# Seven half products for eight in the last 1024 tokens of a forgetting-attention and feed-forward kernel, and a new order of all its operations

## The chip, the cores and the metric

One core of one Trainium2 chip runs the whole program. It has five engines with queues of their own: TensorE (PE in the profile, with PEld for its weight loads), VectorE (DVE), ScalarE (ACT), GpSimd (POOL) and SyncE (SP), which issues most of the DMAs. The metric is the time of the program on the device in microseconds, the median of several runs.

## The reference

Eight batches of eight heads, 576 tokens and 64 channels go through a causal attention with a decay that is a running sum of log f; its output, 4608 tokens of 512 channels, goes through a feed-forward part with two in-projections that are multiplied element by element. In short:

```python
scores = (q @ k.T) / 8 + cum[:, None] - cum[None, :]     # cum = cumsum(log f); -1e9 above the diagonal
attn = softmax(scores)
x = (attn @ v), heads side by side                        # 4608 x 512
a, b = x @ w_a, x @ w_b                                    # 512 x 1536 each
out = (a * b) @ w_out                                      # 1536 x 512
```

## The kernel before

Everything is computed in f16 with f32 sums. The kernel first builds a list of some 2350 operations, each with an engine (or a choice of engines), an assumed duration and what it depends on, and then emits them in an order that is written out in the code: `ORDER` (L1212) is that order, found by a planner, `CHOICE` (L1324) a letter for each operation that may run on more than one engine (D, A, P for DVE, ACT, POOL), and `SLOTS` (L141) the buffer of its ring that each taker of a ring gets. Each engine runs its own operations strictly in that order, so an operation that waits holds all that stands behind it on its engine.

Attention (`attention`, L822) runs for 32 pairs of heads, four to a batch. For a pair: PE forms the scores in PSUM (tile `sc`), DVE adds the decay and takes the row maximum (L674), ACT takes the exponential and its sum (L701, L705), DVE the reciprocal (L713, L715), POOL or ACT multiplies by it (L726, L724; tiles `PA` and `PB`). A DMA transpose issued by SP turns the result (`do_tr`, L736, into `PTA` and `PTB`), PE multiplies it with v (L769, L784, tile `pvx`), and DVE or ACT puts that into `xT`, the feed-forward part's input: four tiles of 128 channels by 4608 tokens. The decay rows (`spread`) come by DMA or by PE.

The feed-forward part (`ffn`, L1124) walks over tiles of tokens, `cuts` (L1206): 256, 256, 256, 384, six of 512, 384. For each of 12 blocks of 128 hidden channels PE forms `psa` and `psb` (`ff_mm`, L1056), ACT copies the first to `a16`, DVE multiplies the second with it into `ht`. A group for 512 tokens is 8 PE instructions, four blocks of 128 input channels in two halves of 64 hidden channels (`mm_halves`, L72). Then, for each 128 tokens, PE forms the output in three groups of 8 (`ff_out`, L1078, tile `pso`), DVE or ACT copies it out, SP stores it. The very last 128 tokens go in three pieces (`psz`). The PSUM ring of the feed-forward part has four buffers (`ff`), that of the scores two of two banks (`sc`).

A tile of `ffn` can start once the attention output of all its tokens is in `xT`. The order spreads these products between the attention's own on PE. "wake" products (L79) fill PE at the start, before there is work for it.

## Time and profile before

| | us |
|---|---|
| runs before | 401.96, 400.78, 397.33 |
| median | 400.78 |
| span of the profiled execution | 397.5 |
| PE busy in it | 386.4 |
| DVE, ACT, POOL busy in it | 293.0, 290.6, 257.8 |

The profiled execution is one of its own; beside its span no time is given for it. In the views, a row of the timeline or of the chain of waits has its start, its length, engine, line, operation, output and inputs, shape and a count; a row of groups has a count, the busy time and the mean of one, and the idle time of the engine in front of them with what ended it; a row of windows has the stretch, then for PE, PEld, DVE, ACT and POOL the busy time with the number of instructions, the granted clock, the share of the DMA engines and GB/s. Nearly all feed-forward products carry the line of their helper, L74, so they are told apart by the tiles' names.

### The profile page before, as it was taken

The numbers are of one execution on the slowest core, as the hardware profiler recorded it, in microseconds if no ns is written. First come the engines' busy times: TensorE is split into PE (matmuls) and PEld (weight loads), VectorE is DVE, ScalarE is ACT, GpSimd is POOL, SyncE is SP. The second block draws the span as 40 slices with busy tenths as digits, with TensorE's granted clock in tenths as the row PEclk, the third lists the DMA queues.
The fourth block names the chain that finished last, engine by engine and source line by source line (L and its number), as shares of the span: only waits on it lengthen the run. The fifth ranks groups of instructions, "written<-read, shape, count | busy, mean of one in ns | idle before, by whom it ended". The sixth has DMA issues, their size and how long they took to land.

```text
span 397.5 us, 14691 instructions
## 1 busy us (share of the span) xinstructions
PE 386.4 (97%) x5768; PEld 250.9 (63%) x5768; DVE 293.0 (74%) x971; ACT 290.6 (73%) x805; POOL 257.8 (65%) x464
## 2 busy tenths in 40 slices
PE   6899999999999999999999999999999999999997
PEld 3557887969766665655555665555555556567785
DVE  7888798999998779787888798668878772333131
ACT  5999899999879778778988588898878763232131
POOL 8689687769887679884996877779936871000000
PEclk9999999999999999999999999999999999999999
DMA  7999999999999999999999999999999586100202
GB/s 117 256 195 167 157 147 226 220 285 283 244 188 228 238 293 234 235 249 292 231 205 278 223 255 214 248 258 206 252 220 230 104 147 156 63 2 1 81 28 81
DMA packets 147365, 76.87 MB, mean 193 GB/s; under 512 B 124384, under 2 KB 128352, under 8 KB 147296
## 3 DMA queue, kind: packets, MB, share of 16 engines
q1 hardware_dynamic: 132856, 68.72, 77.7%
q0 software_dynamic: 14256, 7.08, 14.7%
q8 instruction: 45, 0.74, 0.8%
q14 instruction: 24, 0.20, 0.2%
q10 hardware_dynamic: 184, 0.14, 0.1%
HBM read 52.05 MB, written 9.58 MB: 155 GB/s over the span
## 4 chain that ended last, share of the span: by engine, by line
PE 77%; DMA 11%; POOL 4%; ACT 3%; issue 2%; DVE 2%; SPq 0%; DVEq 0%; ACTq 0%; POOLq 0%
PE psa L74 21%; PE psb L74 20%; PE pso L74 20%; PE sc L551 4%; DMA PTA<-PA 3%; PE pvx L769 3%; POOL PA L726 2%; DMA PTB<-PB 2%; PE psT L359 2%; DMA wb<-in_moe_w_b_dram 2%; PE sc L539 2%; DMA wout<-in_q_dram 2%; PE sc L74 1%; PE psP L74 1%; DMA k<-in_k_dram 1%
## 5 line engine op out<-in xcount | busy, mean ns | idle before, releaser
L674 DVE CUSTOM_DVE_ANT_0 S<-sc,spread 64x576 f32<-64x576 f32 (+4 forms) x232 | 125.9, 562 | 17.3 <-ACT PA L705 8.3
L74 PE MATMUL psb<-xT,wb 128*64 128x512 f16 (+2 forms) x1056 | 113.9, 341 | 0.8 <-DMA wb<-in_moe_w_b_dram 0.5
L74 PE MATMUL psa<-xT,wa 128*64 128x512 f16 (+2 forms) x1056 | 114.1, 341 | 0.0
L289 ACT CAST a<-psa 128x512 f16<-128x512 f32 (+1 forms) x114 | 63.3, 559 | 56.4 <-PE psa L74 52.3
L1073 DVE TENSOR_TENSOR ht<-psb,a 128x512 f16<-128x512 f32 (+1 forms) x114 | 74.4, 658 | 38.5 <-PE psb L74 27.7
L74 PE MATMUL pso<-wout,ht 128*64 128x512 f16 x840 | 102.4, 380 | 0.0
L726 POOL TENSOR_SCALAR PA<-PA,st 128x256 f16<-128x256 f16 (+2 forms) x180 | 84.9, 483 | 8.8 <-DVE st L715 5.5
L705 ACT ACTIVATE PA<-S,st 128x256 f16<-128x256 f32 (+2 forms) x168 | 84.2, 504 | 6.5 <-DVE st L674 6.0
L74 PEld LDWEIGHTS <-wb 128*64 128x64 f16 x1056 | 62.5, 110 | 30.0 <-issue 2.5
L74 PEld LDWEIGHTS <-wa 128*64 128x64 f16 x1056 | 61.7, 110 | 29.3 <-issue 2.2
L726 POOL TENSOR_SCALAR PB<-PB,st 128x512 f16<-128x512 f16 (+1 forms) x90 | 63.4, 711 | 24.3 <-DVE st L715 10.7
L74 PEld LDWEIGHTS <-ht 128*64 128x64 f16 x912 | 49.9, 110 | 33.0 <-issue 1.9
L705 ACT ACTIVATE PB<-S,st 128x512 f16<-128x512 f32 x56 | 40.2, 720 | 3.3 <-DVE st L674 3.0
L705 ACT ACTIVATION_READ_ACCUMULATOR PA<-S,st 128x1 f32 x168 | 32.1, 191 | 0.0
L701 ACT ACTIVATE PB<-S,st 128x576 f16<-128x576 f32 x28 | 21.7, 775 | 9.8 <-POOL PA L726 3.1
L631 POOL TENSOR_SCALAR_AFFINE_SELECT spread<-spread 128x768 f32<-128x768 f32 x24 | 20.9, 870 | 10.1 <-DMA spread<-cum_d 10.0
L769 PEld LDWEIGHTS <-nv 128*64 128x64 f16 x640 | 21.7, 110 | 7.5 <-DMA PTA<-PA 2.1
L674 DVE CUSTOM_DVE_ANT_1 S<-sc,spread 128x256 f32<-128x256 f32 x48 | 19.8, 419 | 6.9 <-PE sc L539 2.0
L715 DVE RECIPROCAL st<-st 128x2 f32<-128x2 f32 x128 | 18.3, 156 | 6.9 <-ACT PB L705 3.5
L674 DVE DVE_READ_ACCUMULATOR2_ANT st<- 128x1 f32 (+1 forms) x280 | 23.0, 82 | 0.0
L551 PE MATMUL sc<-kT,qT 64*128 64x512 f16 (+4 forms) x144 | 20.8, 326 | 1.2 <-ACT kT L289 0.4
L289 ACT COPY osb<-pso 128x512 f32<-128x512 f32 x24 | 13.8, 580 | 9.1 <-PE pso L74 7.8
(106 smaller groups left out, 483.2 us busy)
## 6 DMA issues: line engine op xcount, KB each, us to landing
spread<-cum_d SPq DMA_DIRECT2D x24, 576.0 KB, 6.4
out_dram<-osb SPq DMA_DIRECT2D x35, 256.0 KB, 3.4
q<-in_q_dram SPq DMA_DIRECT2D x14, 576.0 KB, 5.7
k<-in_k_dram SPq DMA_DIRECT2D x14, 576.0 KB, 5.0
v<-in_v_dram SPq DMA_DIRECT2D x24, 256.0 KB, 6.0
wout<-in_moe_w_out_dram POOLq DMA_DIRECT2D x3, 512.0 KB, 7.5
nv<-in_v_dram POOLq DMA_DIRECT2D x8, 128.0 KB, 5.1
wa<-in_moe_w_a_dram POOLq DMA_DIRECT2D x2, 512.0 KB, 7.5
```

The source lines that it names most:

```text
L74: nc.tensor.matmul(out=out[r], lhsT=lhsT[:, r], rhs=rhs, **kw)
L289: nc.scalar.copy(out=out_, in_=in_)
L359: nc.tensor.matmul(out=p[m][HP[j] if quad else slice(0, 128), 64 * t:64 * t + 64], lhsT=x[r, j, t, :] if quad else x[r, t, :], rhs=ident16 ...
L551: nc.tensor.matmul(out=dst, lhsT=lhsT, rhs=rhs, start=start, stop=stop, skip_group_check=True)
L631: nc.gpsimd.affine_select(out=c[:, :, 0:SM].rearrange("p h (j k) -> p h j k", k=128), in_=c[:, :, SM:2 * SM].rearrange("p h (j k) -> p h j ...
L674: nc.vector.tensor_tensor_reduce(out=o, in0=x, in1=y, scale=-1.0, scalar=3e38, op0=ADD, op1=MIN, accum_out=m)
L701: nc.scalar.activation(out=p_blocks(t, 4), in_=T[("s" if direct else "z", t, 4)], func=EXP, bias=st[:, 8:9], scale=sign, accum_out=st[:, 1 ...
L705: nc.scalar.activation(out=p_blocks(t, i)[:, :, h, :], in_=(T[("s", t, i)][:, h, :] if direct else T[("z", t, i)][:, h * n:h * n + n]).rea ...
L715: nc.vector.reciprocal(out=st[:, 20 + 2 * i:22 + 2 * i], in_=st[:, 10 + 2 * i:12 + 2 * i])
L726: VEC[e].tensor_scalar(out=p, in0=p, scalar1=st[:, c:c + 1], scalar2=1.0, op0=MUL, op1=MUL)
L769: nc.tensor.matmul(out=o[HP[h], 128 * i:128 * i + 128], lhsT=vt[:, j, pr + NP * h, :], rhs=pt[:, base_blk[i] + 2 * block_at(t, i, j) + h, ...
L1073: nc.vector.tensor_tensor(out=ht[:, 0:n_], in0=T.pop(("psb", t0, fbs))[:, 0:n_], in1=T.pop(("a16", t0, fbs))[:, 0:n_], op=MUL)
```

## The change

Two things. First, the last 1024 tokens leave `ffn`: `cuts` ends at 3584, as 256, 256, 256, 384, four of 512 and 384, and the rest is done by `winograd()`. There the two weights (rows), the two halves of 512 tokens (columns) and the two halves of the 512 input channels (the inner dimension) are taken as a 2 x 2 block product, and in place of its eight half products seven are formed, from sums of the blocks. Sums of the weights (`sub_w`) are written over parts of `xT` that earlier tiles have used, one of them in place; sums of x (`add_x`) over a fourth part, one in place. The results are put together by copies out of PSUM (`snap`) and by sums and products on DVE and POOL (`combine`). A half product of a block of 128 hidden channels is 4 PE instructions. The output step is the same as before, now a function of its own (`out_step`).

Second, `ORDER`, `CHOICE` and `SLOTS` are all new; with them go other places of the same operations in every queue, and other engines for some. The number of operations goes from 2353 to 2463.

```diff
-    cuts = [256, 256, 256, 384] + [512] * 6 + [384]
+    cuts = [256, 256, 256, 384] + [512] * 4 + [384]
...
+    assert t0 == TW[0]
+    winograd()
...
+    def hidden(t0, fb, tb):
+        if t0 == TW[0]:
+            t0, tb = TW[tb // 4], tb % 4
+        return T[("ht", t0, fb)][:, 128 * tb:128 * tb + 128]
...
+    TW = (NT - 1024, NT - 512)
+    WCOL = 2 * DF
+
+    def w_sum(k):
+        return xTflat[k][:, 0:WCOL].rearrange("p (i c) -> p i c", i=2)
+
+    def x_sum(k, d):
+        c = 512 * (2 * k + d)
+        return xTflat[3][:, c:c + 512]
+
+    def sub_w(e, k, c):
+        a, b = wa16[:, :, c], wb16[:, :, c]
+        out_, x, y = ((w_sum(0), b[:, 0:2], a[:, 0:2]), (w_sum(1), b[:, 2:4], w_sum(0)[:, :, c]),
+                      (w_sum(2), a[:, 2:4], w_sum(1)[:, :, c]), (None, b[:, 2:4], b[:, 0:2]))[k]
+        VEC[e].tensor_tensor(out=b[:, 0:2] if out_ is None else out_[:, :, c], in0=x, in1=y, op=SUB)
+
+    def add_x(e, k, d):
+        p, q_, u, w = (xTflat[m][:, t:t + 512] for m, t in ((d, TW[0]), (2 + d, TW[0]), (d, TW[1]), (2 + d, TW[1])))
+        out_, x, y, op = ((x_sum(0, d), u, w, ADD), (x_sum(1, d), x_sum(0, d), p, SUB),
+                          (u, p, u, SUB), (x_sum(2, d), q_, x_sum(1, d), SUB))[k]
+        VEC[e].tensor_tensor(out=out_, in0=x, in1=y, op=op)
+
+    def product(m, fb):
+
+        f = slice(128 * fb, 128 * fb + 128)
+        if m == 1:
+            T[("wg", fb)] = ff_tile([128, 512], FP32, "wg")
+        if m == 2:
+            T[("wb", fb)] = slot(ps, [128, 2, 512], FP32, "sc", "wb")
+        o = T[("wb", fb)][:, int(m != 2), :] if m in (2, 3, 5) else T[("wg", fb)]
+        for d in range(2):
+            w = {1: wa16[:, d, f], 2: wa16[:, 2 + d, f], 3: wb16[:, 2 + d, f], 4: w_sum(2)[:, d, f],
+                 5: w_sum(0)[:, d, f], 6: w_sum(1)[:, d, f], 7: wb16[:, d, f]}[m]
+            x = {1: xTflat[d][:, TW[0]:TW[0] + 512], 2: xTflat[2 + d][:, TW[0]:TW[0] + 512], 3: x_sum(2, d),
+                 4: xTflat[2 + d][:, TW[1]:TW[1] + 512], 5: x_sum(0, d), 6: x_sum(1, d),
+                 7: xTflat[d][:, TW[1]:TW[1] + 512]}[m]
+            mm_halves(o, w, x, start=(d == 0 and m in (1, 2, 5)), stop=(d == 1), skip_group_check=True)
+
+    def snap(e, m, fb):
+        if m == 1:
+            T[("wu", fb)] = slot(n32_pool, [128, 2 * TG * 64], FP32, "n32", "wu")
+        if m == 5:
+            T[("wv", fb)] = slot(s_pool, [128, 1024], FP32, "S", "wv")
+        c = 512 * (m in (6, 7))
+        cast(e, T[("wu" if m in (1, 6) else "wv", fb)][:, c:c + 512], T[("wb", fb)][:, 1, :] if m == 5 else T[("wg", fb)], False)
+
+    def hidden_tile(half, fb):
+        if half:
+            key, n, tag = ("hx", fb // 3), fb % 3, "PA"
+            if key not in T:
+                T[key] = slot(p_pool, [128, 12, 128], FP16, "PA", "hx")
+        elif fb < 9:
+            key, n = ("hy", fb // 3), fb % 3
+            if key not in T:
+                T[key] = pt_pool.tile([128, 12, 128], FP16, tag="PTA", bufs=RING["PTA"], name="hy")
+        else:
+            x = T[("ht", TW[0], fb)] = slot(ht_pool, [128, 512], FP16, "ht", "ht")
+            return x
+        x = T[("ht", TW[half], fb)] = T[key].rearrange("p n k -> p (n k)")[:, 512 * n:512 * n + 512]
+        return x
+
+    def combine(e, what, fb):
+        u, w, g, be = (T.get((x, fb)) for x in ("wu", "wv", "wg", "wb"))
+        lo, hi = slice(0, 512), slice(512, 1024)
+        out_, x, y, op = {"c11": lambda: (u[:, lo], be[:, 0, :], u[:, lo], ADD),
+                          "c12": lambda: (u[:, hi], be[:, 1, :], u[:, hi], ADD),
+                          "c22": lambda: (w[:, hi], w[:, lo], g if fb in PLAIN else w[:, hi], ADD),
+                          "h1": lambda: (hidden_tile(0, fb), u[:, lo], u[:, hi], MUL),
+                          "h2": lambda: (hidden_tile(1, fb), g, w[:, hi], MUL)}[what]()
+        VEC[e].tensor_tensor(out=out_, in0=x, in1=y, op=op)
+
+    PLAIN = range(0, 12, 2)
+
+    def winograd():
+
+        seen = last_ff["in"]
+        n_in = [0]
+        for n in cuts:
+            n_in.append(n_in[-1] + 2 * 12 // max(1, min(4, 512 // n)))
+        free = [seen[n_in[-2] - 1]]
+        over = [seen[-1]]
+        need = [set(), set()]
+        for half in range(2):
+            for tok in range(TW[half], TW[half] + 512, 64):
+                b, i = tok // S, (tok % S) // 128
+                need[half] |= {ev_ops[(b * NP + pr, i)] for pr in range(NP)}
+        n1, n2 = (sorted(x, key=lambda o: o.n) for x in need)
+        ws, xs = {}, {}
+        for k in range(4):
+            for j in range(3):
+                c = slice(512 * j, 512 * j + 512)
+                ws[(k, j)] = Op("DVE", 0.69, lambda e, k=k, c=c: sub_w(e, k, c),
+                                (over if k == 3 else free) + w_ops[("a", j)] + w_ops[("b", j)] + ([ws[(k - 1, j)]] if k in (1, 2) else [])
+                                + ([ws[(0, j)]] if k == 3 else []), name=f"ws{k}")
+        for k in range(4):
+            for d in range(2):
+                xs[(k, d)] = Op("DVE", 0.45, lambda e, k=k, d=d: add_x(e, k, d),
+                                n1 + n2 + free + ([xs[(k - 1, d)]] if k == 1 else [xs[(0, d)]] if k == 2 else [xs[(1, d)]] if k == 3 else []), name=f"xs{k}")
+        muls = [[], []]
+        hu = {}
+        first = None
+        for fb in range(12):
+            j = fb // 4
+            pr_, sn = {}, {}
+            def mm(m, deps):
+                o = pr_[m] = Op("PE", 4 * 512 * COLS * 0.5 * 1.012, lambda _, m=m, fb=fb: product(m, fb), deps, mode="full", name=f"wm{m}")
+                return o
+            def cp(m, deps=()):
+                o = sn[m] = Op(None, {"ACT": 0.586, "DVE": 0.69}, lambda e, m=m, fb=fb: snap(e, m, fb), [pr_[m], *deps], name=f"snap{m}")
+                return o
+            x = lambda k: [xs[(k, 0)], xs[(k, 1)]]
+            w = lambda k: [ws[(k, j)]]
+            m1 = mm(1, n1 + w_ops[("a", j)] + ([first] if first else []))
+            first = m1
+            gu = take(m1, "ff")
+            m2 = mm(2, n1 + w_ops[("a", j)] + [m1])
+            bu = take(m2, "sc")
+            m5 = mm(5, x(0) + w(0) + [m2])
+            s1 = cp(1)
+            uu = take(s1, "n32")
+            s5 = cp(5, [m2])
+            vu = take(s5, "S")
+            c11 = Op("DVE", 0.69, lambda e, fb=fb: combine(e, "c11", fb), [m2, s1, s5], name="c11")
+            m6 = mm(6, x(1) + w(1) + [s1])
+            s6 = cp(6, [s1])
+            m3 = mm(3, x(3) + w_ops[("b", j)] + [c11])
+            m7 = mm(7, x(2) + w(3) + [s6])
+            if fb in PLAIN:
+                c22 = Op("DVE", 0.69, lambda e, fb=fb: combine(e, "c22", fb), [s5, m7], name="c22")
+                late_ = [c22]
+            else:
+                s7 = cp(7, [s5])
+                c22 = Op("POOL", 1.3, lambda e, fb=fb: combine(e, "c22", fb), [s5, s7], name="c22")
+                late_ = [s7]
+            m4 = mm(4, n2 + w(2) + late_)
+            c12 = Op("DVE", 0.69, lambda e, fb=fb: combine(e, "c12", fb), [m3, s6], name="c12")
+            h1 = Op("POOL", 1.3, lambda e, fb=fb: combine(e, "h1", fb), [c11, c12], name="h1")
+            h2 = Op("DVE", 0.69, lambda e, fb=fb: combine(e, "h2", fb), [m4, c22], name="h2")
+            gu.extend([m6, m7, m4, s1, s6, *late_, h2])
+            bu.extend([m5, s5, c11, m3, c12])
+            uu.extend([s6, c11, c12, h1])
+            vu.extend([*late_, c22, h2])
+            for half, h in ((0, h1), (1, h2)):
+                key = (half, fb if not half and fb >= 9 else fb // 3)
+                if key not in hu:
+                    hu[key] = take(h, "PA" if half else "PTA" if fb < 9 else "ht")
                 else:
-                    uo.append(mo)
-                for _, hu in muls[4 * part:4 * part + 4]:
-                    hu.append(mo)
-                prev = [mo]
-            oc = Op(None, {"ACT": 0.59, "DVE": 0.69}, lambda e, tb=tb: ff_ocopy(e, t0, tb), prev, prio=-2000 + p, name="ocopy")
-            uo.append(oc)
-            ou = take(oc, "osb")
-            so = Op("SP", 0.53, lambda _, tb=tb: ff_store(t0, tb), [oc], prio=-500 + p, land=packets(128, 2048))
-            ou.append(so)
-
+                    h.deps.append(hu[key][0])
+                    hu[key].append(h)
+                muls[half].append((h, hu[key]))
+        for tb in range(8):
+            out_step(TW[0], tb, muls[tb // 4], 0.04 * TW[0])
```

In the new order of PE, the end of attention and the start of `winograd` stand as follows (pv30 and pv31 are the products with v of the last two pairs, pso3200.x.y the output groups of the tile ahead, mK.F half product K of block F):

```
qk30.2 qk31.2 psa3200.6 psb3200.6 psa3200.7 psb3200.7 psa3200.8 psb3200.8 psa3200.9 psb3200.9 pv28
psa3200.10 psb3200.10 psa3200.11 pv29 psb3200.11 pso3200.0.0 pso3200.0.1 pso3200.0.2 pso3200.1.0
pso3200.1.1 pv30 pso3200.1.2 pv31 pso3200.2.0 pso3200.2.1 m1.0 m2.0 m5.0 m1.1 m2.1 m1.2 m6.0
pso3200.2.2 m3.0 m7.0 m6.1 m5.1 m6.2 m4.0 m7.1 m2.2 m3.1 m5.2 m1.3 m7.2 ...
```

More of the change, by code (lines that the diff above doesn't have):

```diff
@@ L1082, in ff_out @@
         for fb in range(4 * part, 4 * part + 4):
-            mm_halves(o, T[("ht", t0, fb)][:, 128 * tb:128 * tb + 128], wout16[:, fb, :],
-                      start=(fb == 0), stop=(fb == 11))
+            mm_halves(o, hidden(t0, fb, tb), wout16[:, fb, :], start=(fb == 0), stop=(fb == 11))
     def ff_ocopy(e, t0, tb):
@@ L1098, in last_out @@
         for fb in range(4 * part, 4 * part + 4):
[L1099 to L1100 removed]
+            mm_halves(o[:, 0:hi - lo], hidden(t0, fb, tb), wout16[:, fb, lo:hi], start=(fb == 0), stop=(fb == 11))
     def last_copy(e, x):
@@ L1179, in ffn @@
-            prev = []
-            for part in range(3):
-                mo = Op("PE", 4 * 512 * COLS * 1.012, lambda _, tb=tb, part=part: ff_out(t0, tb, part),
-                        list(dict.fromkeys(m for m, _ in muls[4 * part:4 * part + 4])) + prev
-                        + w_ops[("o", part)],
-                        prio=5000 + p + 0.1 * part, mode="full", name="pso")
-                chain(mo, "out")
-                if part == 0:
-                    uo = take(mo, "ff")
-                else:
-                    uo.append(mo)
-                for _, hu in muls[4 * part:4 * part + 4]:
-                    hu.append(mo)
-                prev = [mo]
```

140 lines of the change are left out of this document (85 added, 55 removed), and 178 rows, old and new, of the table ORDER.

## The prediction

> **What bounds the kernel now.** I read the page first: span, busy shares, the slices, and the engines of the chain of waits.
>
> ```profile
> span 397.5 us, 14691 instructions
> PE 386.4 (97%) x5768; PEld 250.9 (63%) x5768; DVE 293.0 (74%) x971; ACT 290.6 (73%) x805; POOL 257.8 (65%) x464
> DVE  7888798999998779787888798668878772333131
> POOL 8689687769887679884996877779936871000000
> PEclk9999999999999999999999999999999999999999
> PE 77%; DMA 11%; POOL 4%; ACT 3%; issue 2%; DVE 2%; SPq 0%; DVEq 0%; ACTq 0%; POOLq 0%
> ```
>
> TensorE is busy 97% of the span, at the full granted clock, and carries 77% of the chain. A busy PE is a modelled figure, so I then cut the span at the last attention product (337.14, from the timeline below) and read the table by stage.
>
> ```profile
> 0.00:45.00 45.00, 39.14 (x762) 25.50 (x762) 38.02 (x97) 37.62 (x106) 37.70 (x73) 1.00 1.05 182
> 260.00:337.14 77.14, 77.14 (x1025) 44.13 (x1019) 55.08 (x192) 56.43 (x156) 52.85 (x98) 1.00 0.94 198
> 337.14:394.50 57.36, 57.33 (x636) 40.58 (x628) 17.76 (x29) 15.44 (x30) 0.00 (x0) 1.00 0.11 39
> ```
>
> The columns are PE, PEld, DVE, ACT, POOL. In the first 45 us PE lacks 5.9 us of work (and fills more with idle "wake" products); from then on it is full. Up to 337.14 the others are busy for 68 to 73%, so they have room; after it DVE and ACT are busy under a third of the time and POOL not at all. The kernel is bound by PE's work, which is fed ahead of attention's needs by the feed-forward part. The timeline of PE around the end of attention and at the end:
>
> ```profile
> 320.76 0.61 PE L551 MATMUL sc<-kT,qT 64*128 64x512 f16 x4
> 335.71 0.33 PE L769 MATMUL pvx<-PTA,nv 128*64 128x128 f16 x6
> 336.98 0.32 PE L784 MATMUL pvx<-PTB,nv 128*64 128x64 f16 x10
> 337.14 2.76 PE L74 MATMUL pso<-wout,ht 128*64 128x512 f16 x24
> 350.13 1.05 PE L74 MATMUL psb<-xT,wb 128*64 128x512 f16 x8
> 358.76 1.06 PE L74 MATMUL pso<-wout,ht 128*64 128x512 f16 x8
> 391.63 2.84 PE L74 MATMUL psz<-wout,ht 128*64 128x256 f16 x72
> ```
>
> From 350.13 to 358.76 ten groups of 8 run without a hole: 0.863 us for one group (one of 12 column blocks of one weight, 512 tokens). That is the price of everything below.
>
> **The change, part by part.**
>
> *The removed products.* The last 1024 tokens' two in-projections are 12 x 2 x 2 = 48 groups, or 96 half groups of 4 instructions. The step makes 84. A half group is 0.4315 us, so PE does 12 x 0.4315 = 5.2 us less. All 21 output steps stay at three groups each, and the last in its 72 pieces. Nothing else on PE is added.
>
> *Where that time can appear.* Every product of the step needs the last batch's attention output, for its first token half reaches into that batch. So what stands behind the last attention product becomes: three output groups of the tile ahead (2.6), 84 half groups (36.2), 21 output groups (18.1) and the last pieces (2.7), 59.6 us. Before it is 57.3 us, from the row of windows. So the gain is to be had only if the last attention product ends earlier: 337.14 - 5.2 - 2.3 = 329.6 for all of it, 334.8 for none. In front of it PE has 128 tokens less of both projections to do: 12 x 2 groups of 128 tokens (12 x 2 x 0.216 = 5.2 us) and three output groups (2.6), 7.8 us less. If PE is the bound there, attention moves up by just these 7.8 us, the 7.5 us asked for and a little.
>
> *Can attention move up so far?* I read what is late in it now.
>
> ```profile
> 328.23 3.49 SPq L740 DMA_TRANSPOSE PTB<-PB  x2
> 328.86 1.36 POOL L726 TENSOR_SCALAR PB<-PB,st 128x512 f16<-128x512 f16 x2 [0.66 <-DVE st L715]
> PTB<-PB SPq DMA_TRANSPOSE x28, 5.2
> ```
>
> The last normalization ends at 330.22; of the two transposes issued one after the other from 328.23 the second starts near 330, and lands 5.2 us later, about 335.2; the products that read it start at 335.71. So from the last scores (320.76) to them there is a chain of 15.0 us, and PE work without a hole covers it. In the new order I count on PE between the same two operations 12 groups of 384 tokens (12 x 0.65), three attention products (1.9) and six output groups (5.2), 14.9 us behind the scores' own 0.6: the same cover. A hole of up to 1 us may open there; I take 0, since the chain is unchanged and its vector work has 29% of room.
>
> *Twelve weight subtractions and eight sums of x on DVE.* Nine of twelve subtractions (1024 elements a partition, f16, both inputs in SBUF) stand in DVE's order ahead of the last attention product, the rest and the eight sums (512 elements) behind it. No row shows such an operation. The nearest:
>
> ```profile
> L1073 DVE TENSOR_TENSOR ht<-psb,a 128x512 f16<-128x512 f32 x90 | 61.4, 686 | 23.4 <-PE psb L74 15.5 <-ACT a L289 7.1
> L293 DVE COPY xT<-psP 128x768 f16<-128x768 f16 x10 | 5.4, 552 | 0.7 <-PE psP L74 0.6
> ```
>
> A subtraction costs between 0.55 (fewer elements, one input) and 1.37 us (twice the row of 512); I take 0.7, as the f16 row is the nearer type. Nine of them: 6.3 us (4.9 to 12.4) in a stage where DVE stands idle 22 of 77 us, so they hide, and cost their own 6.3 us only where DVE's queue has no hole: queued behind one is the next row maximum, then its exponential on ACT and the normalization. The sums: 0.4 (0.35 to 0.69) each. The first two must stand between the eviction of the last attention output and the third product; that eviction (0.75) and two sums (0.8) lie beside two output groups and two products (2.6 us). Hidden, with 1 us over.
>
> *The vector operations of the product stretch.* Where two copies on ACT and two products on DVE stood for a column block there are now three or four copies out of PSUM and five combinations. From the letters of the choice table 34 of the 42 copies go to ACT and 8 to DVE; of the 60 combinations 42 are DVE's and 18 POOL's.
>
> ```profile
> 344.31 1.07 ACT L289 CAST a<-psa 128x512 f16<-128x512 f32 x2 [2.92 <-PE psa L74]
> 345.42 1.29 DVE L1073 TENSOR_TENSOR ht<-psb,a 128x512 f16<-128x512 f32 x2 [2.99 <-ACT a L289]
> L726 POOL TENSOR_SCALAR PB<-PB,st 128x512 f16<-128x512 f16 x61 | 42.1, 694 | 15.9 <-DVE st L715 10.7 <-ACT PA L705 2.1 <-issue 1.7
> L293 POOL CAST k<-k 128x1152 f16<-128x1152 f32 x14 | 16.0, 1143 | 2.2 <-DMA k<-in_k_dram 1.8 <-PE psT L359 0.3
> ```
>
> Two DVE products in a row take 1.29, so the second starts 0.60 after the first. DVE then needs 52 x 0.60 (combinations, copies, two output copies), 8 x 0.4 and 3 x 0.7: 36.5 us back to back, 52 x 0.69 + 5.3 = 41.2 us if each waits by itself. It has the 84 half groups and the five output groups that PE runs between them, 40.5 us, less 0.9 for the last eviction: 39.6 us. ACT needs 34 x 0.55 = 19. POOL's 18 two-input operations cost between 0.69 and 2.29 us (two casts of 1152); at 1.39, two of the f16 row, 25 us of 40. The chain inside a block (copy 0.58, combination 0.69, product 0.43, combination 0.69, with about 0.1 each to be noticed) is 4 us for the two-buffer PSUM ring, against 6.0 us of PE work for two blocks. So PE is the bound in this stretch too, with DVE 3 us behind it at best and 1.6 us ahead at worst. PE loses 0 to 4 us; I take 0.4, three restarts at the price that the chain of waits shows for one (0.98 against 0.86):
>
> ```profile
> 205.14 0.98 PE psa L74 x8
> 206.12 0.86 PE psb L74 x8
> ```
>
> [...]
>
> *The new order of everything else.* The same attention operations, some moved between DVE, ACT and POOL; one weight load is issued ahead of the first loads of v in POOL's queue and three right behind them, earlier than now. PE's work is the same, all 24 wake products are kept. What it can win is the 5.9 us that PE lacks in the first 45 us, what it can lose is as much; between -3 and +3 I take 0.
>
> *Sum.* -5.2 + 0.4 = -4.8 us against a span of 397.5: a span of 392.7. No time is known of the profiled execution but its span; the median of the runs shown is 400.78, 3.3 above it, and the runs lie from 397.33 to 401.96. Against the median: 400.78 - 4.8 = 396.0 us, 1.2% faster. About 1% is what a measurement of this kernel can tell from no change.
>
> **The rivals.**
>
> *Attention doesn't move up (slower).* Its end is set by its own chain and not by PE: the last products start half a us after their transposes land, and nine subtractions stand in DVE's queue in front of the last reciprocals or the maxima before them. For it: that coincidence, and the 15.0 us chain. Against it: DVE, ACT and POOL each idle over a quarter of that stage, and the cover of PE work in front of the last product is as long as before. Its point: the last attention product later than 334.8 - 0.4 = 334.4. At the old 337.14 the span grows by 2.3 + 0.4 to 400.2, time 403.5; with 2 us of subtractions in front, 405.5.
>
> *DVE becomes the bound of the product stretch.* If every one of its operations pays 0.69 and the in-order queue waits for the wrong block now and then, PE loses the upper bound of 4 us: 396.0 + 3.6 = 399.6. For it: 41.2 of 39.6 us. Against it: the 0.60 spacing.
>
> [...]
>
> *The replay pays by itself.* Half of what PE lacks in the first 45 us goes: 396.0 - 3 = 393.0. For it: the earlier weight loads; against it: DVE, ACT and POOL are busy there for 84% already.
>
> **How the numbers follow.** My forecast 0.52, with a range of its own of 394.0 to 398.5; attention stays 0.14; DVE bound 0.13; blocking 0.07; the replay pays 0.14. The bound of 1% is 396.8: about 0.65 of the forecast's chance lies below it, 0.34, and all of the replay's 0.14: faster 0.48. Slower by over 1% (404.8) is half of the first rival, 0.07, and 0.03 for a worse start. The rest, 0.42, is within 1%. The range goes from below the replay's case to short of the old attention end: 390.5 to 402.5.
>
> **What would show it.** Right: the last attention product ends by about 329 to 330, the half groups follow each other every 0.43 us, the 336 instructions of the seven products take some 36.7 us of PE, and 59.6 to 61 us lie between the last attention product and the last matmul. Wrong in attention: that product stays later than 334 while DVE shows the subtractions just ahead of the maxima. Wrong in the stretch: over 62 us behind it, and PE waiting for DVE's combinations. Blocking: subtractions well over 0.7 us, or normalizations longer than 0.69. Wrong altogether: PE doesn't have 48 instructions less (5720), or the granted clock leaves 1.00.

## The result, and the profile after

The changed kernel takes 402.58 us (median of 20 runs, 399.97 to 408.1) where the kernel before takes 399.79 on the same chip (20 runs, 397.01 to 402.71). The ratio is 1.0077, with a 95% interval of 1.0054 to 1.0100: slower by 0.8%, which is less than the 1% at which the prediction drew its line but clear of no change, and not 1.2% faster as forecast. The profiled execution of it has a span of 398.4 us, against 397.5 before; it took 400.45 us, 2.1 less than the median, so its rows show rather less of the loss than a usual execution would. The ratios, here and in the experiments, leave out executions more than 1.5% slower than the fastest of the same kernel, among them four of the six of the kernel at 1.0761 below, and the only profiled one (988 us) of the kernel with the old order to 200 us.

The page of the changed kernel: its span, TensorE's share and count, the granted clock in 40 slices, the chain by engine.

```profile
span 398.4 us, 14685 instructions
PE 385.1 (97%) x5720; PEld 250.3 (63%) x5720; DVE 322.6 (81%) x1022; ACT 292.0 (73%) x807; POOL 283.0 (71%) x485
PEclk9899999999999999999999999999999999999999
PE 71%; DMA 8%; DVE 7%; POOL 6%; issue 4%; ACT 3%; SPq 0%; POOLq 0%; ACTq 0%; DVEq 0%
```

The 48 instructions are gone (5768 to 5720), and TensorE is still busy 97%. But its share of the chain that ended last fell from 77% to 71%, and DVE, POOL and issue, 8% together before, now hold 17%. The table by stage, cut at the end of the attention again:

```profile
0.00:45.00 45.00, 39.91 (x754) 25.68 (x756) 38.46 (x100) 37.08 (x104) 39.16 (x75) 0.96 1.13 199
260.00:335.47 75.47, 74.78 (x1075) 47.44 (x1071) 64.92 (x219) 58.29 (x169) 57.58 (x102) 1.00 1.04 213
335.47:395.20 59.73, 59.73 (x606) 39.77 (x601) 38.97 (x64) 21.83 (x41) 22.69 (x18) 1.00 0.11 41
```

TensorE's timeline where the attention ends, the first half groups of the seven products, and the last pieces:

```profile
335.32 0.35 PE L783 MATMUL pvx<-PTB,nv 128*64 128x64 f16 x10
335.47 1.92 PE L74 MATMUL pso<-wout,ht 128*64 128x512 f16 x16
337.20 0.63 PE L74 MATMUL wg<-xT,wa 128*64 128x512 f16 x4
337.63 0.62 PE L74 MATMUL wb<-xT,wa 128*64 128x512 f16 x4
338.07 0.63 PE L74 MATMUL wb<-xT,xT 128*64 128x512 f16 x4
...
392.73 2.84 PE L74 MATMUL psz<-wout,hx 128*64 128x256 f16 x72
```

Half groups follow each other every 0.43 us, and from 335.47 to the last matmul's end at 395.57 TensorE has no idle time in the table. That is 60.1 us behind the last attention product, and the prediction counted 59.6 and 0.4 for restarts. So the seven products do what was worked out for them. What failed lies in front: the last attention product is over at 335.47, and was to be over at 329.6. The same stretch before ended at 337.14. With 7.8 us less for TensorE to do in front of that point it came 1.7 us earlier; 6 us went missing between 0 and 335 us. The same stage table for the stretches between shows only a part of them as idle time:

```profile
45.00:145.00 100.00, 97.84 (x1818) 74.13 (x1816) 85.51 (x312) 87.52 (x248) 72.64 (x125) 1.00 1.02 218
145.00:200.00 55.00, 52.91 (x704) 29.53 (x702) 43.84 (x156) 44.10 (x128) 44.15 (x81) 1.00 1.03 233
200.00:290.00 90.00, 89.49 (x1190) 49.98 (x1188) 75.44 (x263) 69.39 (x196) 69.55 (x127) 1.00 1.07 236
```

TensorE idles 2.16, 2.09 and 0.51 us there; in the kernel before the same stretches have 1.25, 0.92 and 0.00. That is 2.6 us more, spread over all three. The busy time hides short holes, which is also why it stays at 97%:

```profile
L74 PE MATMUL pso<-wout,ht 128*64 128x512 f16 x696 | 84.9, 380 | 0.0
```

One product is shown 0.38 us long, while in a full stretch eight of them take 0.863 us, one every 0.108; a short hole between two counts as busy.

The granted clock leaves 1.00 once while TensorE has work: the table has 0.96 for the first 45 us. All of that lies in one stretch, which begins in a hole of 1.03 us:

```profile
12.31:15.72 3.41, 3.10 (x63) 1.89 (x65) 2.77 (x6) 2.06 (x9) 3.37 (x6) 0.50 1.05 405
12.62 0.50 PE L550 MATMUL sc<-kT,qT 64*128 64x256 f16 x4 [1.03 <-DVE kT L292]
```

The kernel before has 1.00 there.

### The profile page after: what moved, and what is told of

Its sections match the earlier page's. It is cut to its first block, busy times and chain, and to the rows that moved or that the text cites. A ratio compares the mean times of both kernels' runs of the same rounds, so it can differ in the third digit from the quotient of the medians.

```text
span 398.4 us, 14685 instructions
## 1 busy us (share of the span) xinstructions
PE 385.1 (97%) x5720; PEld 250.3 (63%) x5720; DVE 322.6 (81%) x1022; ACT 292.0 (73%) x807; POOL 283.0 (71%) x485
## 4 chain that ended last, share of the span: by engine, by line
PE 71%; DMA 8%; DVE 7%; POOL 6%; issue 4%; ACT 3%; SPq 0%; POOLq 0%; ACTq 0%; DVEq 0%
PE pso L74 18%; PE psa L74 13%; PE psb L74 12%; PE wg L74 5%; PE sc L550 4%; PE wb L74 4%; DVE S L673 4%; DMA PTB<-PB 3%; PE pvx L768 3%; PE psP L74 2%; POOL PA L725 2%; PE wake L74 2%; POOL PB L725 2%; DMA q<-in_q_dram 2%; PE psT L358 2%
## 5 line engine op out<-in xcount | busy, mean ns | idle before, releaser
L673 DVE CUSTOM_DVE_ANT_0 S<-sc,spread 64x576 f32<-64x576 f32 (+4 forms) x232 | 125.3, 561 | 14.7 <-POOL spread L637 3.1
L725 POOL TENSOR_SCALAR PA<-PA,st 128x256 f16<-128x256 f16 (+2 forms) x181 | 84.4, 477 | 12.1 <-DVE st L714 6.6
L74 PE MATMUL psa<-xT,wa 128*64 128x512 f16 (+2 forms) x864 | 88.7, 333 | 2.9 <-DVE st L673 1.8
L74 PE MATMUL psb<-xT,wb 128*64 128x512 f16 (+2 forms) x864 | 88.7, 333 | 0.7 <-ACT a L288 0.6
L725 POOL TENSOR_SCALAR PB<-PB,st 128x512 f16<-128x512 f16 (+1 forms) x91 | 65.6, 727 | 27.7 <-DVE st L714 10.3
L74 PE MATMUL pso<-wout,ht 128*64 128x512 f16 x696 | 84.9, 380 | 0.0
L74 PEld LDWEIGHTS <-wa 128*64 128x64 f16 x960 | 54.8, 110 | 30.2 <-issue 3.9
L74 PEld LDWEIGHTS <-wb 128*64 128x64 f16 x960 | 54.9, 110 | 25.5 <-issue 3.0
L1072 DVE TENSOR_TENSOR ht<-psb,a 128x512 f16<-128x512 f32 (+1 forms) x90 | 57.4, 648 | 9.3 <-PE psb L74 5.0
L288 ACT CAST a<-psa 128x512 f16<-128x512 f32 (+1 forms) x90 | 48.9, 548 | 16.4 <-PE psa L74 15.1
L74 PEld LDWEIGHTS <-ht 128*64 128x64 f16 x696 | 39.5, 110 | 26.7 <-issue 2.0
L1273 POOL TENSOR_TENSOR hy<-wu 128x512 f16<-128x512 f32 x9 | 11.5, 1278 | 18.6 <-DVE wu L1273 18.5
L673 DVE CUSTOM_DVE_ANT_1 S<-sc,spread 128x256 f32<-128x256 f32 x48 | 19.6, 419 | 6.3 <-PE sc L538 2.4
L292 DVE COPY osb<-pso 128x512 f32<-128x512 f32 x18 | 12.3, 686 | 14.1 <-PE pso L74 13.6
L673 DVE DVE_READ_ACCUMULATOR2_ANT st<- 128x1 f32 (+1 forms) x280 | 22.7, 81 | 0.0
```

Of the source, the lines that this page charges most:

```text
L74: nc.tensor.matmul(out=out[r], lhsT=lhsT[:, r], rhs=rhs, **kw)
L288: nc.scalar.copy(out=out_, in_=in_)
L292: VEC[e].tensor_copy(out=out_, in_=in_)
L673: nc.vector.tensor_tensor_reduce(out=o, in0=x, in1=y, scale=-1.0, scalar=3e38, op0=ADD, op1=MIN, accum_out=m)
L725: VEC[e].tensor_scalar(out=p, in0=p, scalar1=st[:, c:c + 1], scalar2=1.0, op0=MUL, op1=MUL)
L1072: nc.vector.tensor_tensor(out=ht[:, 0:n_], in0=T.pop(("psb", t0, fbs))[:, 0:n_], in1=T.pop(("a16", t0, fbs))[:, 0:n_], op=MUL)
```

## The experiments

Four explanations stood against each other: A, the order of the attention found anew loses the time; B, with 128 tokens less of feed-forward work in front of it the attention is the bound by itself, in any order; C, subtractions and sums block GpSimd and through it the last head pairs. D came up later: one late mask in GpSimd's queue. Ratios are to the kernel before, run beside each on the same chip; 1% is 4 us. Each kernel ran 6 or 12 times (the changed kernel 20), in groups on different chips, and the changed kernel wasn't run again in these groups, so a step of a few tenths of a per cent between two rows of different groups is not to be leaned on.

| kernel | ratio | 95% interval |
|---|---|---|
| changed kernel | 1.0077 | 1.0054 to 1.0100 |
| old order to 145 us | 1.0022 | 0.9992 to 1.0051 |
| old order to 200 us | 0.9929 | 0.9898 to 0.996 |
| old order to 250 us | 0.9985 | 0.9953 to 1.0016 |
| old order to 290 us | 0.9889 | 0.9847 to 0.993 |
| old order from 145 to 290 us | 1.0055 | 1.0023 to 1.0086 |
| new order, no seven products | 1.017 | 1.0125 to 1.0216 |
| no subtractions, no sums | 1.0044 | 1.001 to 1.0079 |
| SP's old sequence alone | 1.0439 | 1.0391 to 1.0486 |
| old choice of engines alone | 1.0364 | 1.0316 to 1.0411 |
| old four engines, SP's new sequence | 1.0761 | 1.067 to 1.0851 |
| old in all five queues | 1.0341 | 1.0282 to 1.04 |
| mask of pair 14 earlier, new order | 1.0063 | 1.0026 to 1.0101 |
| mask of pair 14 later, old order to 290 us | 1.0009 | 0.9978 to 1.0041 |
| 14 masks earlier, new order | 1.0105 | 1.0069 to 1.0141 |

### The order and the seven products taken apart

The first 2144 operations (all of the attention, the feed-forward tiles to token 3200) are the same in both kernels, with the same numbers. So an order can be grafted: to a chosen point the old one, then what is left in the new one, where both have done the same operations but for 2 to 5. In the changed kernel:

```diff
     ORDER = """
-        46 0-2 5 6 29 3 30 31 7 8 52 32 62 53 47 37 38 33 34 36 48 35 50 54 9 39 40 4 56 44 82 58 42 63 85 64
+        0 1 29 30 46 2 52 62 5 3 31 37 32 38 33-36 39 40 42 41 53 47 58 4 43 267 262 279 6-9 54 48
...
```

> The changed kernel with its last 1024 tokens by seven half products as they are, and the order, the choice of engines and the ring slots of the kernel before for the first 1800 of the operations that both kernels have (to about 290 us); behind that the changed kernel's order. Theory A (the order found anew loses the time, in the attention in front of the product stretch): the last attention product comes back to about 330 us and the whole to 5 or 6 us under the changed kernel, ratio to the kernel before 0.990 to 0.997. Theory B (with 128 tokens less of feed-forward work in front of its end, the attention itself is the bound, whatever the order): as the changed kernel, ratio 1.004 to 1.011. Theory C (subtractions and sums hold GpSimd, and so the last head pairs, up): as the changed kernel too, since they are where they were.

Measured 0.9889. Its end of the attention on TensorE, and its last pieces:

```profile
331.29 0.35 PE L784 MATMUL pvx<-PTB,nv 128*64 128x64 f16 x10
331.44 1.92 PE L74 MATMUL pso<-wout,ht 128*64 128x512 f16 x16
...
389.24 2.84 PE L74 MATMUL psz<-wout,hx 128*64 128x256 f16 x72
```

The last attention product is over at 331.44, 4 us before that of the changed kernel, and 60.6 us lie behind it. The work in front is the same and the subtractions are where they were: B and C fall as the cause of these 4 us, A stands (its ratio is even a little below the 0.990 that A gave). This kernel also beats both, with 396.7 us beside 400.67.

The reverse, the kernel before with the new order up to the last attention eviction and its own tiles of 512 and 384 tokens behind it:

```diff
     ORDER = """
-        0 1 29 30 46 2 52 62 5 3 31 37 32 38 33-36 39 40 42 41 53 47 58 4 43 267 262 279 6-9 54 48
+        46 0-2 5 6 29 3 30 31 7 8 52 32 62 53 47 37 38 33 34 36 48 35 50 54 9 39 40 4 56 44 82 58 42
...
```

> The kernel before with all its tiles of 512 and 384 tokens (no seven products, no subtractions or sums), but with the changed kernel's order, choice of engines and slots up to the last attention eviction; behind that the order of the kernel before. Theory A: the loss of 5.8 us at the last attention product stays and nothing pays for it, ratio to the kernel before 1.010 to 1.018. Theory B: the 128 tokens that cover the attention's end are back and the order is harmless, ratio 0.997 to 1.004. Theory C: with no subtraction and no sum anywhere the loss is gone, 0.997 to 1.004 too.

Measured 1.017. With before and after this makes a square of two orders and two ways to do the last 1024 tokens; it is not quite even, as one corner has the old order to 290 us and the other the new one to the end of the attention. The new order costs 1.7% without the seven products and 1.9% with them (0.9889 to 1.0077), 6.8 and 7.5 us. The seven products win 1.1% under the old order (1 to 0.9889) and 0.9% under the new (1.017 to 1.0077), 4.4 and 3.7 us, where 4.8 was forecast. What they won the order took, and more. The four profiles show a part of it in one stretch, 120 to 200 us; the kernels are before, changed, old order to 290 us, new order without seven products. The second column is TensorE's busy time and its instructions.

```profile
120.00:200.00 80.00, 78.10 (x1084) 47.35 (x1080) 65.88 (x242) 65.97 (x192) 63.00 (x114) 1.00 1.13 250
```

```profile
120.00:200.00 80.00, 76.38 (x1060) 44.77 (x1058) 62.93 (x230) 63.39 (x185) 59.92 (x109) 1.00 1.05 238
```

```profile
120.00:200.00 80.00, 78.45 (x1092) 47.99 (x1090) 66.66 (x245) 66.14 (x193) 63.01 (x114) 1.00 1.11 253
```

```profile
120.00:200.00 80.00, 75.13 (x1026) 43.88 (x1026) 60.56 (x224) 59.52 (x175) 56.48 (x104) 0.98 0.99 227
```

With the old order TensorE idles 1.6 to 1.9 us of the 80, with the new 3.6 and 4.9. All of the other engines do less too: none of them has become the bound.

The subtractions and sums left out (`sub_w` and `add_x` emit nothing):

```diff
     def sub_w(e, k, c):
+        return
...
     def add_x(e, k, d):
+        return
```

> The changed kernel without the twelve subtractions of weights and the eight sums of tokens: their instructions are left out, the half products read what stands in those places. [...] Theories A and B: the loss stands far in front of them, and at most 1 us comes back, ratio 1.004 to 1.010.

Measured 1.0044, inside the ratio of A and B. It is 0.3% or 1.3 us under the changed kernel, where A and B allowed 1 us and C asks for most of the 6 us that went missing, and the intervals overlap. So they cost about 1.3 us, if anything, and are not the loss.

### Where between 0 and 290 us

The same graft at other points, and the old order only between two of them.

```diff
     ORDER = """
         46 0-2 5 6 29 3 30 31 7 8 52 32 62 53 47 37 38 33 34 36 48 35 50 54 9 39 40 4 56 44 82 58 42
...
-        <the new order from the 906th to the 1800th shared operation>
+        <the old order for them>
```

> As the kernel with the old order to about 290 us, but the old order holds only for the first 905 of the shared operations (to about 145 us). The two traces differ by 2.2 us at the product of head pair 10 and by 3.9 us at that of head pair 12, which stand about there. Theory A: what was lost in front of the seam comes back and no more, 2 to 4 us, ratio to the kernel before 0.997 to 1.003. Theory B: as the changed kernel, 1.004 to 1.011. If the new order behind the seam only fits what stood in front of it, the seam costs something too and less than 2 us come back.

> The changed kernel's order to the 905th shared operation (about 145 us), the order before from there to the 1800th (about 290 us), then the changed kernel's. The old order to 145 us alone was worth 0.55% (1.0077 to 1.0022), the old order to 290 us 1.9% (to 0.989). If the loss gathers piece by piece, this kernel wins the other 1.3%, ratio 0.992 to 0.998. If the long hole at 153 us, behind the seam, is the fruit of what stands in front of it, it stays: 1.000 to 1.008.

> The changed kernel with the old order for the first 1250 of the shared operations, to about 200 us. Known: the old order for 0, 905 and 1800 of them gives ratios of 1.0077, 1.0022 and 0.989 to the kernel before. If one stretch between 145 and 200 us (with the hole at 153) holds most of the rest: 0.988 to 0.995. If the loss gathers evenly to 290 us: 0.994 to 1.001. If what matters is only that no seam lies where the load is tight: no order in the four numbers.

> The same with 1705 shared operations, to about 250 us. If most of the rest is between 145 and 200 us: as the graft at 290 us, 0.986 to 0.992. If the loss gathers evenly: 0.989 to 0.996. If the last 40 us in front of 290 us matter by themselves: 0.996 to 1.002.

Measured 1.0022, 1.0055, 0.9929 and 0.9985. The old order to 145 us gives 2.2 us back, to 200 us 5.9, to 290 us 7.5: most of the loss lies in front of 200 us. Three results don't fit a plain sum. The graft at 250 us is 2.2 us worse than that at 200. It falls into the range of "the last 40 us matter by themselves", but then the graft at 200 us, which lacks them too, should not be at 0.9929; that a seam has a price of its own would explain it and isn't tested. The stretch from 145 to 290 us in the old order gives back only 0.9 us when the new order stands in front of it, and 5.3 (1.0022 to 0.9889) when the old one does. And that kernel's 1.0055 falls into the range of "the hole at 153 us stays", but the hole is gone: its timeline of TensorE has none from 148 to 162 us. The graft at 145 us still has one there, of 1.71 us, and isn't the slower of the two.

A part of the first 2.2 us may be the start. Seven of the eight profiles that begin in the new order have a stretch of 3.41 us at half the granted clock, from somewhere between 12.3 and 14.6 us on (0.96 for the first 45 us in each); of those that begin in the old order none has. TensorE does 728 to 754 instructions in the first 45 us of these seven, and 762 to 780 in the five profiles that keep the kernel before's order and engines there (the kernel before, the grafts at 145, 250 and 290 us, and the late mask). At 45 us for 762 instructions, some 26 to 36 fewer are an estimate of up to 2 us. No run takes this apart from the rest.

### Which queue

> The changed kernel with one queue put back: SP issues the loads, transposes and stores that both kernels have in the sequence of the kernel before; the sequences of the other four engines and the choice of engines are the changed kernel's. Theory A1 (the transfers, moved by the new order, come late and hold GpSimd up: its waits for k, q and v went from 3.8 to 11.4 us): most of the 5 to 7 us that the old order is worth comes back, ratio to the kernel before 0.989 to 0.998. Theory A2 (the sequences of the four engines lose it, the transfers only follow): nothing comes back, 1.004 to 1.012. Theory A3 (66 operations on another engine): as A2.

> The mirror of it: the four computing engines run the shared operations in the sequence and on the engines of the kernel before, and only SP's queue has the changed kernel's sequence. The last 1024 tokens go by seven half products. A1: the loss is there, ratio to the kernel before 1.002 to 1.012. A2 and A3: the loss is gone, 0.986 to 0.994, as the kernel with the old order to about 290 us (0.989).

> The changed kernel with its own sequence of all operations, but each of the 66 shared operations that has another engine in it is put back on the engine of the kernel before (evictions, transposes' copies and normalizations between VectorE, ScalarE and GpSimd). A3: 5 to 7 us come back, ratio to the kernel before 0.989 to 0.998. A1 and A2: 1.003 to 1.012.

SP's operations, 161 in all, of which 80 stand at another place (the second kernel has the reverse):

```diff
-    262 500 274 279 1735 512 507 495 332 ...
+    262 279 274 500 1735 495 512 332 505 ...
```

The third has 66 other letters:

```diff
     CHOICE = """
-        DDPDADADADADPPPPPPAPPDADDAPPPPAPAAADDDPPPPAAPPPDAAAPPAAAPPPPDDDDADDDAAAADDPAPPPAPPPDAAAPPPAPPAPAADDDPPP
+        DDDDADADADAAPPAPPPAPPAADAPPPPPPAPADDDDPPPAPPPPPDDDDPAAPAPPPADDDADAADAAAADDPPPAPAPPPADDAAPPAPPAPAADAD
...
```

Measured 1.0439, 1.0761 and 1.0364. All three hypotheses miss, in the same way: no part gives the time back, and SP's old sequence and the old engines, each put into the new order, make it worse by some 3% (1.0077 to 1.0439 and 1.0364: 14.5 and 11.5 us). So these runs don't tell which part of the new order loses the time. The first 45 us of the kernel with the old choice of engines:

```profile
0.00:45.00 45.00, 36.74 (x698) 23.63 (x700) 35.63 (x92) 34.29 (x97) 37.12 (x72) 1.00 1.09 191
```

TensorE does 698 instructions there, against 754. It looks as if sequence, engines and transfers were fitted to each other; what is shown is that none of these exchanges could be made alone.

```diff
     ORDER = """
-        46 0-2 5 6 29 3 30 31 7 8 52 32 62 53 47 37 38 33 34 36 48 35 50 54 9 39 40 4 56 44 82 58 42 63 85 64
+        46 0-2 5 6 29 3 30 31 7 8 52 32 62 53 47 37 38 33-36 9 54 48 39 40 56 50 44 58 4 42 41 45 43
...
```

> The seven half products with everything of the old order that can be kept: all shared operations on the sequence and the engines of the kernel before in all five queues, to the end of the attention, not only to 290 us. Theory A: at least what the graft at 290 us gave, ratio 0.984 to 0.991. If the new order of the last head pairs is what moves the attention's end up in front of the product stretch, this one is slower than that graft: 0.991 to 1.000.

Measured 1.0341, where the graft at 290 us has 0.9889. This kernel and the one with SP's new sequence were built queue by queue, and in both the operations of the tile at token 3200, which are not shared, stand at the new order's places among old neighbours, and some ring buffers are others. So they don't test what they were to test. Beside each other they say only that SP's new sequence costs about 4% (1.0761, of two executions, to 1.0341) where the four other engines have the old one.

### One mask in GpSimd's queue

The longest wait of TensorE in the changed kernel's profile behind the start:

```profile
152.33 1.03 PE L74 MATMUL psb<-xT,wb 128*64 128x512 f16 x8
154.92 1.05 PE L74 MATMUL psa<-xT,wa 128*64 128x512 f16 x8 [1.56 <-DVE st L673]
```

Its chain of waits, from the load of a pair's decay rows to this product:

```profile
139.67 0.42 SPq L338
...
140.19 6.83 DMA spread<-cum_d
...
147.14 0.44 POOL spread L630
...
148.00 1.61 POOL PA L725 x4
149.61 0.67 POOL PB L725
150.28 1.81 POOL PA L725 x4
152.09 0.67 POOL PB L725
152.76 0.37 POOL spread L637
153.15 0.69 DVE S L673
...
154.92 1.05 PE psa L74 x8
```

The load lands at 147.02. GpSimd then copies the mask of pair 15 (L630), runs ten normalizations (L725), and only then the mask of pair 14's last diagonal block (L637), for which VectorE waits with its decay (L673), and behind that with the product that frees TensorE's PSUM buffer. The normalizations wait for nobody; they are just ahead in the queue. In the kernel before, GpSimd's timeline at this place:

```profile
145.70 0.87 POOL L631 TENSOR_SCALAR_AFFINE_SELECT spread<-spread 128x768 f32<-128x768 f32 x1 [1.33 <-DMA spread<-cum_d]
146.56 0.69 POOL L726 TENSOR_SCALAR PB<-PB,st 128x512 f16<-128x512 f16 x1
147.23 1.39 POOL L726 TENSOR_SCALAR PA<-PA,st 128x384 f16<-128x384 f16 x3
148.58 0.40 POOL L638 TENSOR_SCALAR_AFFINE_SELECT spread<-spread 128x256 f32<-128x256 f32 x1
```

Four stand between, and the mask runs 4.2 us earlier; 1.4 of that is the mask copy in front, which starts at 145.70 in place of 147.14. Moving the one operation (813), in the changed kernel up past six normalizations, in the graft at 290 us six normalizations ahead of it:

```diff
-    779 804 741 743 805 925 1867 ... 822 ... 749 794 ... 786 813
+    779 804 741 743 813 805 925 1867 ... 822 ... 749 794 ... 786
```

```diff
-    742 813 844 862 ... 787 743 779 799 806 ... 794
+    742 787 743 779 799 806 794 813 844 862
```

> The changed kernel with one of its 2463 operations moved: the mask of head pair 14's last diagonal block (0.4 us on GpSimd) goes up past six normalizations in GpSimd's queue, to where four stand between it and the mask copy of pair 15, as in the kernel before; ten stand there in the changed kernel. Theory D (the long hole of TensorE at 153 us is the end of a chain through that queue: load of the decay rows, mask copy, ten normalizations, mask, decay on VectorE, product on VectorE, PSUM buffer): the mask runs near 149 us in place of 152.7 and the hole of 1.6 us is gone or under 0.4, and 1 to 2 us come back, ratio to the kernel before 1.002 to 1.006. Rival E (VectorE is simply full there): the hole stays above 1 us, ratio 1.005 to 1.010.

> The reverse, in the kernel with the old order to about 290 us: six normalizations of GpSimd's queue are put ahead of the same mask, so that ten stand before it. Theory D: the mask ends some 3.5 us later, VectorE waits for it, and a hole of 0.5 to 2 us opens on TensorE near 150 us which that kernel doesn't have; ratio to the kernel before 0.991 to 0.996 in place of 0.989. Rival E: no hole and no difference, 0.986 to 0.991.

GpSimd's and TensorE's timelines with the mask earlier:

```profile
149.94 0.41 POOL L638 TENSOR_SCALAR_AFFINE_SELECT spread<-spread 128x256 f32<-128x256 f32 x1
```

```profile
153.66 1.03 PE L74 MATMUL psb<-xT,wb 128*64 128x512 f16 x8
154.65 1.05 PE L74 MATMUL psa<-xT,wa 128*64 128x512 f16 x8
```

And with it later: GpSimd, VectorE, TensorE.

```profile
152.17 0.41 POOL L638 TENSOR_SCALAR_AFFINE_SELECT spread<-spread 128x256 f32<-128x256 f32 x1
```

```profile
152.61 0.69 DVE L674 CUSTOM_DVE_ANT_0 S<-sc,spread 128x512 f32<-128x512 f32 x1 [3.57 <-POOL spread L638]
```

```profile
149.02 1.05 PE L74 MATMUL psa<-xT,wa 128*64 128x512 f16 x8
153.71 1.92 PE L74 MATMUL psb<-xT,wb 128*64 128x512 f16 x8 [3.63 <-DVE st L674]
155.37 0.74 PE L74 MATMUL sc<-kT,qd 128*64 128x512 f16 x4
```

The chain is shown from both sides: the hole goes with the mask earlier and opens, 3.63 us long, with it later. The price is not the same on both sides. Later costs 1.2% (0.9889 to 1.0009), 4.8 us: D's hole of 0.5 to 2 us and its ratio were both too small, for the hole is longer and slower products follow it (eight in 1.92 us, below). Earlier gives 1.0063 against 1.0077, no difference that can be told, and just outside D's 1.002 to 1.006; by the time alone E isn't excluded, by the hole it is. With the hole of 1.56 us gone the last attention product of that execution is over no earlier, at 336.48 (single executions differ by as much as this 1 us), so what is gained at this place seems to be waited for elsewhere.

Two of the 14 masks moved up together (operations 611 and 1129):

```diff
-    ... 578 699 708 611 659 ... 1186 1089 1069 1129 1986
+    ... 613 698 578 611 699 708 ... 1009 1983 1025 1129 1174 1172
```

> The changed kernel with 14 of its masks of last diagonal blocks moved up in GpSimd's queue by 1 to 9 operations, to the second place behind the maxima that they must follow. If masks that stand too late behind normalizations are the new order's general fault, most of its loss comes back: ratio 0.990 to 0.998. If only that of pair 14 is late, as ml14_up: 1.002 to 1.006. If normalizations that now run later hold ScalarE's and SP's transposes up, slower than the changed kernel: over 1.010.

Measured 1.0105: late masks are not the general fault of the new order. That it is worse than the changed kernel isn't shown, as the intervals overlap.

## Why the prediction was wrong

- *The seven products:* right. The half group takes 0.43 us, 84 of them run without a hole in the table, TensorE has 5720 instructions, and the step is worth 3.7 to 4.4 us (forecast 4.8).
- *Behind the last attention product:* right; 60.0 with the restarts, measured 60.1.
- *The end of the attention:* "a hole of up to 1 us may open there; I take 0". TensorE's idle time from 260 to 335.47 us is 0.7 us in the table by stage. Within its bound.
- *The operations' durations:* the subtraction was taken at 0.7 us and takes 0.67 to 1.06; the sum at 0.4, 0.42; GpSimd's two-input operation at 1.39, 1.27 to 1.28. VectorE is busy 39.0 us behind the last attention product, inside the 36.5 to 41.2, and by the table by stage TensorE has no idle time there: it didn't become the bound. The rows of the changed kernel by group:

```profile
L1218 DVE TENSOR_TENSOR xT<-wb,xT 128x1024 f16<-128x1024 f16 x3 | 3.0, 990 | 0.1
L1218 DVE TENSOR_TENSOR xT<-wa,xT 128x1024 f16<-128x1024 f16 x3 | 2.0, 679 | 0.0
L1224 DVE TENSOR_TENSOR xT<-xT,xT 128x512 f16<-128x512 f16 x5 | 2.1, 423 | 3.0 <-ACT xT L288 3.0
```

```profile
L1273 POOL TENSOR_TENSOR hy<-wu 128x512 f16<-128x512 f32 x9 | 11.5, 1278 | 18.6 <-DVE wu L1273 18.5
```

- *Sums and readings.* "From then on it is full" had no row for 45 to 260 us: TensorE idles 1.25 us from 45 to 145 and 0.92 from 145 to 200, so it was nearly full. The chain inside a block, given as 4 us, adds up to 2.8 from its own terms (of them the 0.1 for each start behind the end it waits for is 0.04 for ACT's copy at 346.04 and 0.10 for DVE's product at 346.97 in the timeline before), and the upper bound of 4 us that PE may lose there isn't worked out (41.2 less 39.6 is 1.6). "All 21 output steps stay at three groups each" means seven steps of three groups, and the sum counts them so. None of this moves the forecast.
- *The step that failed* is "the new order of everything else": "PE's work is the same ... What it can win is the 5.9 us that PE lacks in the first 45 us, what it can lose is as much; between -3 and +3 I take 0." It costs 6.8 to 7.5 us. The bound was drawn from one stretch only. Up to 2 us by the estimate above are lost in that stretch, where the clock also left 1.00 (0.96), a sign that the prediction had named; the rest is lost behind it, where TensorE was nearly full and a new order had little to win, while the idle time of the old order is no bound on what it can lose: there the queues of the other engines decide how long a hole gets, as the late mask shows (3.63 us behind six normalizations more). With it fell "if PE is the bound there, attention moves up by just these 7.8 us": PE no longer was, for 6 us in all. Even in the graft at 290 us the last attention product is over at 331.44 and not at 329.6; that 1.8 us isn't explained.
- *The rivals.* "Attention doesn't move up" gave 403.5, near the 402.58 measured, but for another reason. Its chain of 15.0 us and its subtractions are all in the graft at 290 us, where the attention ends at 331.44. "The replay pays by itself" had the sign wrong. Of blocking, to which it gave 0.07, a little is true: both of its signs, "subtractions well over 0.7 us, or normalizations longer than 0.69", are in the changed kernel's timelines. Three subtractions that run beside normalizations or a mask on GpSimd (at 318.40, 325.18 and 329.02) take 0.92 to 1.06 us. The other nine take 0.67 to 0.80, and four of those run beside some too (0.80 at 295.01, 0.76 at 321.26, 0.67 at 326.55, 0.78 at 328.20). Three of the four normalizations from 326.73 to 330.64 take 1.05 to 1.12 us, the fourth 0.69. But it is not the loss: without any subtraction and sum 1.3 us come back.

What stays open: most of the 7 us has been placed (in front of 200 us) and not been put down to single waits. The one wait that was followed to its source is real, and its removal alone doesn't shorten the run by anything that can be told. How much of the first 2.2 us is the start at half clock wasn't tried. Why the stretch from 145 to 290 us is worth 0.9 us behind the one beginning and 5.3 behind the other isn't settled either; the late loads of q and k that GpSimd waits for weren't tried by themselves.

## What to carry to other kernels

A change that comes with a new order is two changes: graft the old order in front of the new part, before judging the part. Where the bounding engine is nearly full, a new order has little to win and may lose far more, so give that term a one-sided range; and look for the loss in the in-order queues of the engines that are not full, by counting what stands between a transfer's first user and the operation that the bounding engine waits for. Don't exchange one queue's sequence or the choice of engines in a fitted order: here that cost about 3 to 4% each time. And don't take a busy share of 97% for a proof that nothing is lost.

## What was not expected of the hardware

A hole on TensorE cost more than its length in some of these kernels, and not in others. After the hole of 1.56 us in the changed kernel the next eight instructions take 1.05 us, as without a hole. After 3.63 us with the late mask they take 1.92. The new order without the seven products has one too, at the place of the 1.56:

```profile
158.07 1.92 PE L74 MATMUL psa<-xT,wa 128*64 128x512 f16 x8 [3.16 <-DVE st L674]
159.78 1.69 PE L74 MATMUL psb<-xT,wb 128*64 128x512 f16 x8
161.30 0.41 PE L74 MATMUL sc<-kT,qd 128*64 128x512 f16 x4
```

There the pace is back some 3 us later, with the late mask after 5. In the stretch from 140 to 160 us of the kernel with the late mask the granted clock is 0.83 in the table by stage; it is 0.50 from 152.05 to 158.88, 6.83 us, and 1.00 in the rest:

```profile
140.00:160.00 20.00, 16.33 (x138) 9.46 (x139) 12.30 (x47) 11.69 (x37) 14.92 (x27) 0.83 1.17 252
```

The length of the hole alone doesn't decide. The 1.03 us at the start of the changed kernel go with 3.41 us at half clock, and so do 2.03 us in the kernel with SP's old sequence, while 1.56 and 1.71 us near 154 us, and 1.02 at the start of the kernel with the old choice of engines, do not:

```profile
177.16 0.36 PE L769 MATMUL pvx<-PTA,nv 128*64 128x128 f16 x6 [2.03 <-DVE st L674]
```

The two stretches at half clock that are given with their ends last 3.41 us and 6.83, twice as long; what starts and what ends one, no run shows.
